# Turning q and k by transposing transfers instead of matmuls, in an attention kernel with an ELU block

## The chip, the cores and the metric

The kernel runs on one core of a Trainium2 chip. The metric is the device time of one execution in microseconds (us), as the median of several runs; lower is better.

A core has engines that each run their own instructions in order and wait for each other by semaphores. The profile calls them PE (TensorE, matmuls; its loads of stationary operands are the row PEld), DVE (VectorE), ACT (ScalarE), POOL (GpSimd) and SP (SyncE, which here only issues transfers). Transfers (DMAs) run beside them on 16 DMA engines, through one queue for SP and one for POOL. PE writes its results to PSUM, 8 banks of 2 KB in each of 128 partitions; all other on-chip data lies in SBUF.

## The reference, cut to what matters

Two attentions are computed on the same q, k and v and added: one on tokens averaged in groups of 4, whose output rows are repeated 4 times, and one local, in which a token sees only tokens at a distance under 4. The sum goes through two dense layers with an ELU between them.

```python
B, H, S, D = 8, 8, 576, 64            # batch, heads, tokens, head size
q_d = q.reshape(B, H, S // 4, 4, D).mean(axis=3)       # k_d, v_d likewise
out_up = np.repeat(sm_attn(q_d, k_d, v_d), 4, axis=2)
mask = np.abs(pos[:, None] - pos[None, :]) < 4
out_local = softmax(where(mask, q @ k.T / 8, -1e9)) @ v
x = (out_up + out_local).transpose(0, 2, 1, 3).reshape(4608, 512)
h = x @ w_in                           # 512 -> 2048
g = np.where(h > 0, h, np.exp(np.minimum(h, 0)) - 1)
return g @ w_out                       # 2048 -> 512
```

## The kernel before, in words

**Attention.** The work is cut by batch b (8) and by pair of heads j (4 in a batch). For each pair, q and k come from HBM by one transfer each into a tile `ld` (float32: 96 partitions, 2 heads, 6 blocks of 96 tokens, 64 wide). POOL casts each into a tile `c16` of 16-bit floats, in the order block, head, width (line 516). A score needs q and k with the head's width on the partitions, so each block of 96 x 128 has to be turned. Before, PE does that: a matmul with the block as the stationary operand and a constant as the moving one. The constant `ONE` has 120 columns, an identity of 96 and 24 columns that average 4 tokens each, so the same matmul also gives the averaged tokens (line 548, batches 2 to 7). ACT then copies the result from PSUM into the tiles `qt` (128 x 720), `kt` and `kd` (lines 563, 575 and 577). Batches 0 and 1 (`SIX`) load their tokens in another order, 6 neighbouring tokens on one partition, with longer pieces in HBM, and are turned with other constants (lines 536 and 540; evictions 571 and 572).

From `qt`, `kt` and `kd`, PE computes the scores: 12 matmuls for the local windows (line 620) and 4 for the averaged tokens (line 628). ACT takes the exponential of both heads (line 637), DVE multiplies with a band mask (line 644). Once a batch, PE sums the denominators with constant matrices (line 665), DVE takes the reciprocal (line 692), and from batch 2 on POOL spreads it over the partitions through a DRAM tile `rd` into `rcb` (lines 719 and 724). PE multiplies the weights with v (lines 748 and 756), DVE normalizes into `xn` (line 771), and POOL adds local and averaged outputs into `xt`, the operand of the dense layers (line 787). v is loaded into one tile of float32 and cast by POOL (lines 470 and 473).

**Dense layers.** The 4608 tokens are cut into 9 tiles of 512. A tile has 16 groups `mm1` of 4 matmuls (line 804), each followed by an exponential on ACT (line 810) and two passes on DVE (812, and 815 which writes `gt`), and 16 groups `mm2` of 4 matmuls (line 827), whose results ACT copies to `os` (842) and SP stores (845). Tile t needs the attention output of the batches whose tokens it holds: the last two tiles need batch 7.

**What sets the order.** Every operation is recorded with its engine, an assumed duration, its buffers and a rank, a due time in the units of the assumed durations. A planner (`Plan.run`) then plays the engines forward: each engine takes, among the operations that are ready and whose buffers are free, the one of lowest rank. The order that comes out is written into the program, engine by engine; on the chip each engine runs it in that order, whatever the real durations are. Ranks come from the numbers in `PARAM`: dense tile t is due from `M0 + P * t` on, the pair j of batch b from `late(b, j) = M0 + P * b - LEAD + GAP * j` on. A pair's casts have the rank `late` - 8, its transposes `late`, its scores `late` + `SC` (3.9 before), its loads `late` - `LOAD` (23.14); a batch's outputs are due `OUT` (1.4 before) ahead of the tile.

The planner also deals out the buffers (`SLOTS`): 8 of `ld`, 4 of `c16`, 3 each of `qt` and `kt` (with a `kd` each), and the PSUM banks. A pair of banks ("two") is taken by a transposed operand, by the scores of one head and by the outputs of one pair; in steady state only banks 0 to 3 serve these, and 4 to 7 the dense layers, at most 3 for `mm1` and 2 for `mm2`. SP may have 8 transfers open at a time: each waits for the one eight places earlier.

Of the kernel before, what the change touches and what calls it, by code (L numbers as in the profile page):

```python
# [11 lines left out]
FP32 = mybir.dt.float32  # L12
AB = mybir.AluOpType
AF = mybir.ActivationFunctionType

B, H, S, D = 8, 8, 576, 64
SD = S // 4
SCALE = 0.125
NB, QB = 6, 96
KW = QB + 6  # L20
VB = 112
HB = 3 * QB
# [47 lines left out]
class Plan:  # L70
# [183 lines left out]
    def emit(self):  # L254
        for o in self.order:
# [5 lines left out]
    "rcb": 2, "rc": 2, "rd": 2, "xn": 3, "xt": 3, "gt": 2, "e": 4, "os": 3,  # L261
}
MOE_BANKS = {"hp": 3, "op": 2}
PARAM = dict(M0=30, P=36.77, LAG=1.06, LEAD=53.49, GAP=7.69, SC=3.9, DEN=33.04, OUT=1.4, OUTG=1.98,
             LOAD=23.14, VLOAD=27.91, VCAST=36.99, warm=3.4, FILL=27.63, WI=-27.58, WO=38.12, WOG=2.24,
             OVER=1.0, LEAD1=57.82, GAP1=5.57, OUT1=32, VLOAD1=41.43, LOAD1=28.31, CC=-45.43, tv0=-26.96,
             C0=-7.99, SC0=2.71, OUTA=-25.9, OUTB=-21.42, DEN0=3.42, DENB=-28.86, SPA=-26.1, SPB=-20.87,
             V0=-46.5, G0=1, G1=2, G2=3, G3=3, G4=3, G5=8, G6=3, G7=13, G8=13, L0=2, L1=6, L2=0, L3=8,
             L4=0, LAG0=1.07, QG=2.08)


@with_exitstack
def kernel(
# [15 lines left out]
    def many(kind, shape, dt=FP16):  # L289
# [25 lines left out]
    def at(b):  # L315
        return T[b.kind][b.slot[0]]
# [36 lines left out]
    def fills():  # L353
        for t, x in (("ONE", 0.0), ("BY6", 0.25), ("VR", 0.25), ("MASK", 1.0), ("IND", 0.0), ("FIRST", 1.0), ("GAP", 0.0)):
            nc.vector.memset(C[t][:], x)  # L355
        nc.vector.memset(C["ONE"][:, QB:], 0.25)
        nc.vector.memset(C["VR"][:, 24:], 0.0)
        nc.vector.memset(C["IND"][:, 9:10], 1.0)
        nc.vector.memset(C["FIRST"][:, 1:10], 0.0)
        for i in range(3):  # L360
            nc.vector.memset(C["GAP"][32 * i : 32 * i + 24, 9:10], 1.0)
        for t in T["kt"]:
            nc.vector.memset(t[:, 0:3], 0.0)
            nc.vector.memset(t[:, S + 3 : S + 6], 0.0)
        for t in KD:
            nc.vector.memset(t[:], 0.0)

# [139 lines left out]
    def cast(b, j):  # L507
        s, r = st[b, j], late(b, j)
        s["c"], s["op"] = [], []
        for i, x in enumerate(s["ld"]):  # L510
# [9 lines left out]
            )  # L520
            s["c"].append(y)

    def transposes(b, j):
        s, r = st[b, j], late(b, j)
        yq, yk = s["c"]
        m = b in SIX
        con = c_a
        for which, y in (("q", yq), ("k", yk)):
            z = Buf("two", b < EARLY)

            def go(y=y, z=z):
                t = at(y)

                def natural(c):
                    o = PS[:, z.slot[0] + c // 3, 96 * (c % 3) : 96 * (c % 3) + 96]
                    nc.tensor.matmul(o, t[:, c, :, :], C["ONE"][:, 0:QB], start=True, stop=True)

                for c in range(NB):
                    if m:
                        nc.tensor.matmul(  # L540
                            PS[:, z.slot[0] + 1, HB : HB + SD], t[:, c, :, :], C["BY6"][:, c],
                            start=(c == 0), stop=(c == NB - 1),
                        )
                        if c < 3:
                            natural(c)
                    else:
                        o = PS[:, z.slot[0] + c // 3, 120 * (c % 3) : 120 * (c % 3) + 120]
                        nc.tensor.matmul(o, t[:, c, :, :], C["ONE"][:], start=True, stop=True)  # L548
                for c in range(3, NB) if m else ():
                    natural(c)  # L550

            op("PE", 0.63 if m else 0.315, r + (0 if which == "q" else 0.2), go, reads=[y], writes=[z],
               after=[con], name=f"t{which}{b}{j}")
            w = Buf("qt" if which == "q" else "kt")

            eng = "DVE" if b == 0 and which == "k" else "ACT"

            def ev(z=z, w=w, which=which, copy=nc.vector.tensor_copy if eng == "DVE" else nc.scalar.copy):
                zz = PS[:, z.slot[0], 0:1]
                if which == "q":  # L560
                    t = at(w)
                    if not m:
                        copy(  # L563
                            out=t[:].rearrange("p (g u) -> p g u", g=2), in_=_free(zz, [[512, 2], [1, 360]])
                        )
                        return
                    o, od = t[:, 0:1], t[:, S : S + 1]
                else:
                    o, od = at(w)[:, 3:4], KD[w.slot[0]][:, 0:1]
                if m:  # L570
                    copy(out=_free(o, [[1, 2 * 3 * QB]]), in_=_free(zz, [[1, QB], [512, 2], [QB, 3]]))
                    copy(out=_free(od, [[1, SD]] if which == "q" else [[32, NB], [1, 24]]),
                         in_=PS[:, z.slot[0] + 1, HB : HB + SD])
                    return
                copy(out=_free(o, [[HB, 2], [96, 3], [1, 96]]), in_=_free(zz, [[512, 2], [120, 3], [1, 96]]))  # L575
                zp = PS[:, z.slot[0], 96:97]
                copy(out=_free(od, [[QB, 2], [32, 3], [1, 24]]), in_=_free(zp, [[512, 2], [120, 3], [1, 24]]))

            op(eng, (0.72 if which == "q" else 0.9) if not m else 0.97 if eng == "DVE" else 0.86, r + 0.3, ev, reads=[z], writes=[w],
               after=[o_fill], name=f"ev{which}{b}{j}")  # L580
            s[which] = w

# [24 lines left out]

    def scores(b, j):
        s, r = st[b, j], late(b, j) + (PARAM["SC"] if b else PARAM["SC0"])
        m = b in SIX  # L610
        qb, kb = s["q"], s["k"]
        sc = [Buf("two", b < EARLY), Buf("two", b < EARLY)]

        def go():
            qt, kt, kd = at(qb), at(kb), KD[kb.slot[0]]
            for c in range(NB):
                for e in range(2):
                    p = slice(64 * e, 64 * e + 64)
                    qa = QB * c if m else 120 * c
# [309 lines left out]
```

## Time and profile before

| what | value |
|---|---|
| runs, median (lowest to highest) | 363.8 us (362.5 to 365.24, 3 runs) |
| the profiled execution, span from first to last instruction | 362.9 us; the page gives no other time of it |
| mean granted TensorE clock | 0.984 of full |
| packets on SP's queue | 108,038, 39.49 MB, 52.3% of 16 engines' span |
| packets on POOL's queue | 6,288, 8.84 MB, 13.3% |
| loads of q and k (64 in all) | 288 KB each, 5.2 and 5.4 us from issue to landing (median) |
| stores of the output (36) | 256 KB each, 2.0 us to landing |
| DVE waiting for the exponential (line 644 for 637) | 41.4 us in 28 waits |
| DVE waiting for the outputs' matmuls (line 771 for 756) | 23.8 us in 8 waits |
| SP waiting for ACT's copy to `os` before a store | 169.0 us in 30 waits |

A row of a group in the profile names line, engine, operation, output and inputs, shape and count; then the busy time of the group in us, the mean time of one in ns, and the idle time of the engine just before, with what ended it. The busy time counts overlapping instructions once, so for pipelined matmuls it is less than count times mean. "DMA" in the rows by slice is the mean busy share of the 16 DMA engines in tenths, one digit for each fortieth of the span (9.07 us); in the windows the share can exceed 1, since packets on one engine overlap. The chain of waits follows back from the last instruction to what released it, step by step.

### The profile page before, as it was taken

The numbers are of one execution on the slowest core, as the hardware profiler recorded it, in microseconds if no ns is written. First come the engines' busy times: TensorE is split into PE (matmuls) and PEld (weight loads), VectorE is DVE, ScalarE is ACT, GpSimd is POOL, SyncE is SP. The second block draws the span as 40 slices with busy tenths as digits, with TensorE's granted clock in tenths as the row PEclk, the third lists the DMA queues.
The fourth block names the chain that finished last, engine by engine and source line by source line (L and its number), as shares of the span: only waits on it lengthen the run. The fifth ranks groups of instructions, "written<-read, shape, count | busy, mean of one in ns | idle before, by whom it ended". The sixth has DMA issues, their size and how long they took to land.

```text
span 362.9 us, 8968 instructions
## 1 busy us (share of the span) xinstructions
PE 347.5 (96%) x3677; PEld 189.3 (52%) x3677; DVE 224.4 (62%) x410; ACT 211.5 (58%) x364; POOL 144.0 (40%) x226
## 2 busy tenths in 40 slices
PE   8995999999998998999999999999999999999995
PEld 7984554455454554554555455555554444444442
DVE  3658598336885597557755865398547667765510
ACT  2643696469865677557855785488557415544411
POOL 7645554277274544570557055634330160000000
PEclk9998799899999999999999999999999999999999
DMA  8999999999979799479746975103001311010021
GB/s 218 216 157 225 258 199 191 202 201 235 234 168 222 193 181 220 93 157 214 155 94 153 218 149 99 61 35 83 31 30 60 87 48 40 0 58 33 29 77 68
DMA packets 114366, 48.89 MB, mean 135 GB/s; under 512 B 100662, under 2 KB 108662, under 8 KB 114326
## 3 DMA queue, kind: packets, MB, share of 16 engines
q1 hardware_dynamic: 108038, 39.49, 52.3%
q0 software_dynamic: 6288, 8.84, 13.3%
q8 instruction: 28, 0.46, 0.6%
q14 instruction: 12, 0.10, 0.1%
HBM read 42.86 MB, written 9.66 MB: 145 GB/s over the span
## 4 chain that ended last, share of the span: by engine, by line
PE 78%; DVE 9%; ACT 6%; issue 2%; DMA 2%; POOL 2%; ACTq 0%; DVEq 0%; POOLq 0%
PE bank L827 32%; PE bank L804 27%; PE bank L548 4%; PE bank L620 3%; PE bank L748 3%; DVE e L812 3%; PE bank L329 3%; ACT e L810 2%; DVE gt L815 2%; PE bank L665 2%; ACT ex L637 2%; DVE ex L644 2%; DMA rcb<-rd 1%; PE bank L540 1%; PE bank L756 1%
## 5 line engine op out<-in xcount | busy, mean ns | idle before, releaser
L804 PE MATMUL bank<-xt,WI 128*128 128x512 f16 x576 | 141.2, 382 | 1.6 <-DVE gt L815 1.4
L827 PE MATMUL bank<-WO,gt 128*128 128x512 f16 x576 | 140.3, 381 | 1.9 <-DVE gt L815 1.9
L810 ACT ACTIVATE e<-bank 128x512 f16<-128x512 f32 x144 | 85.1, 603 | 49.1 <-PE bank L804 27.2
L815 DVE SCALAR_TENSOR_TENSOR gt<-bank,e 128x512 f16<-128x512 f32 x144 | 97.8, 688 | 4.9
L827 PEld LDWEIGHTS <-gt 128*128 128x128 f16 x576 | 54.0, 98 | 64.4 <-DVE gt L815 2.6
L804 PEld LDWEIGHTS <-WI 128*128 128x128 f16 x576 | 53.1, 98 | 64.0 <-issue 6.3
L812 DVE TENSOR_SCALAR e<-e 128x512 f16<-128x512 f16 x144 | 55.4, 386 | 39.6 <-ACT e L810 38.8
L516 POOL CAST c<-ld 96x768 f16<-96x768 f32 x60 | 50.6, 861 | 50.5 <-issue 25.7
L637 ACT ACTIVATE ex<-bank 102x864 f16<-102x864 f32 x64 | 53.4, 887 | 23.7 <-PE bank L628 23.5
L787 POOL TENSOR_TENSOR xt<-xn 128x288 f16<-128x288 f16 (+8 forms) x92 | 44.4, 514 | 54.1 <-DVE xn L771 54.0
L644 DVE TENSOR_TENSOR ex<-ex,MASK 102x1152 f16<-102x1152 f16 x32 | 28.6, 895 | 41.5 <-ACT ex L637 41.4
L842 ACT COPY os<-bank 128x512 f32<-128x512 f32 x36 | 21.3, 590 | 46.4 <-PE bank L827 43.4
L771 DVE TENSOR_TENSOR xn<-bank,rcb 128x720 f16<-128x720 f32 x32 | 27.8, 901 | 25.6 <-PE bank L756 23.8
L473 POOL CAST v<-v 102x768 f16<-102x768 f32 x32 | 27.5, 887 | 0.3 <-DMA v<-in_v_dram 0.3
L548 PEld LDWEIGHTS <-c 96*128 96x128 f16 x288 | 18.1, 97 | 8.0 <-issue 0.4
L563 ACT CAST qt<-bank 128x720 f16<-128x720 f32 x24 | 18.3, 761 | 4.2 <-PE bank L548 3.7
L548 PE MATMUL bank<-ONE,c 96*128 96x120 f16 x288 | 20.6, 216 | 0.0
L719 POOL DMA_DIRECT2D rd<-rc x6 | 3.5, 578 | 41.3 <-DVE rc L692 19.7
L329 PE MATMUL bank<-zero 128*128 128x128 f16 x221 | 17.3, 240 | 1.8 <-DVE ONE L355 1.1
L620 PEld LDWEIGHTS <-kt 64*102 64x102 f16 x384 | 11.7, 125 | 12.6 <-ACT e L810 4.7
L575 ACT CAST kt<-bank 128x576 f16<-128x576 f32 x24 | 15.6, 651 | 1.2 <-ACT qt L563 1.2
L329 PEld LDWEIGHTS <-zero 128*128 128x128 f16 x221 | 15.1, 109 | 2.4 <-DVE zero L332 1.1
(67 smaller groups left out, 228.6 us busy)
## 6 DMA issues: line engine op xcount, KB each, us to landing
ld<-in_q_dram SPq DMA_DIRECT2D x32, 288.0 KB, 5.2
ld<-in_k_dram SPq DMA_DIRECT2D x32, 288.0 KB, 5.4
out_dram<-os SPq DMA_DIRECT2D x36, 256.0 KB, 2.0
v<-in_v_dram SPq DMA_DIRECT2D x13, 672.0 KB, 8.8
rcb<-rd POOLq DMA_DIRECT2D x12, 360.0 KB, 5.6
WO<-in_moe_w_out_dram POOLq DMA_DIRECT2D x4, 512.0 KB, 9.1
WI<-in_moe_w_in_dram POOLq DMA_DIRECT2D x3, 512.0 KB, 11.3
v<-in_v_dram SPq DMA_DIRECT2D x3, 336.0 KB, 8.6
```

The costliest lines, as they stand in the source:

```text
L329: nc.tensor.matmul(PS[:, 7, 384:512], zero[:, 0:128], zero[:, 128:256], start=True, stop=True)
L516: f(out=at(y)[:], in_=at(x)[:].rearrange("p e c d -> p c e d"))
L548: nc.tensor.matmul(o, t[:, c, :, :], C["ONE"][:], start=True, stop=True)
L637: lambda e=e: nc.scalar.activation(out=at(x)[:, e], in_=two(sc[e], 0, KW, 0, HB + SD), func=AF.Exp, scale=SCALE),
L644: nc.vector.tensor_tensor(out=a, in0=a, in1=mk, op=AB.mult)
L771: lambda: nc.vector.tensor_tensor(out=at(w)[:], in0=two(z, 0, 128, 0, GW), in1=at(y)[:, j], op=AB.mult),
L787: (nc.vector if eng == "DVE" else nc.gpsimd).tensor_tensor(out=at(xt(t))[:, j, o : o + n - a], in0=ln, in1=gn, op=AB.add)
L804: nc.tensor.matmul(one(h, 0, 128, 0, TBLK), WI[:, dc, 128 * fc : 128 * fc + 128], at(x)[:, dc, :], start=(dc == 0), stop=(dc == DMC - 1),)
L810: op("ACT", 0.55, r, lambda: nc.scalar.activation(out=at(e)[:], in_=one(h, 0, 128, 0, TBLK), func=AF.Exp), reads=[h], writes=[e], name=f"e ...
L812: op("DVE", 0.42, r, lambda: nc.vector.tensor_scalar(out=at(e)[:], in0=at(e)[:], scalar1=1.0, scalar2=-1.0, op0=AB.min, op1=AB.add), reads ...
L815: op("DVE", 0.64, r, lambda: nc.vector.scalar_tensor_tensor(out=at(gt)[:, fc, :], in0=one(h, 0, 128, 0, TBLK), scalar=0.0, op0=AB.max, in1 ...
L827: nc.tensor.matmul(one(z, 0, 128, 0, DM), at(gt)[:, fc, 128 * tt : 128 * tt + 128], WO[:, fc, :], start=(fc == 0), stop=(fc == FCN - 1),)
```

## The change

From batch 2 on, q and k are no longer turned by PE. For each of them SP issues one transposing transfer from the cast tile `c16` (96 partitions, 768 elements) straight into `qt` or `kt` (128 partitions, 6 blocks of 96), both in SBUF. The averaged tokens no longer come out of the same step: DVE sums 4 neighbouring tokens, for q into the last 144 columns of `qt`, for k into `kd`, and scales all of `kd` by 1/16, which stands for both averages. The matmuls of line 548 and the copies of lines 563, 575 and 577 are gone, and with them the PSUM banks that they took. Batches 0 and 1 are turned as before.

`kt` gets a margin of `KO` = 16 columns instead of 3 on each side, zeroed at the start, so that the transfer's target is aligned; the scores read from it accordingly, and `qt` now has its 576 tokens in one piece. The transfers have the rank `late` + `TU` (-5), the sums 1.0 more. The score rank `SC` goes from 3.9 to 8.25 (batch 1 too), the outputs' lead `OUT` from 1.4 to 5.0, that of batch 1 (`OUT1`) from 32 to 26.86; the last part of `w_out` waits for an earlier cast (`G8` from 13 to 4); `VCAST` and `WO` move by under 0.3.

```diff
+KO = 16
-PARAM = dict(M0=30, ..., SC=3.9, DEN=33.04, OUT=1.4, ..., VCAST=36.99, ..., WO=38.12, ..., OUT1=32, ..., G8=13, ...)
+PARAM = dict(M0=30, ..., SC=8.25, DEN=33.04, OUT=5.0, ..., VCAST=36.92, ..., WO=38.35, ..., OUT1=26.86, ..., G8=4, ..., TU=-5.0)
...
-        "kt": many("kt", [128, S + 6]),
+        "kt": many("kt", [128, S + 2 * KO]),
...
+    def turned(b, j):
+        s, r = st[b, j], late(b, j) + PARAM["TU"]
+        for i, (which, y) in enumerate(zip("qk", s["c"])):
+            w = Buf("qt" if which == "q" else "kt")
+
+            def go(y=y, w=w, which=which):
+                t = at(w)
+                a = t[:, 0:S] if which == "q" else t[:, KO : KO + S]
+                nc.sync.dma_start_transpose(
+                    out=a.rearrange("p (c u) -> p c u", c=NB), in_=at(y)[:].rearrange("p c e d -> p (c e d)"))
+
+            op("SP", 1.5, r + 0.1 * i, go, reads=[y], writes=[w], nbytes=S * 256, rate=200e3, packet=75,
+               after=[o_fill], name=f"tu{which}{b}{j}")
+
+            def pool(w=w, which=which):
+                t = at(w)
+                if which == "q":
+                    nc.vector.tensor_reduce(out=t[:, S : S + SD], in_=t[:, 0:S].rearrange("p (u f) -> p u f", f=4),
+                                            axis=AX.X, op=AB.add)
+                    return
+                d = _free(KD[w.slot[0]][:, 0:1], [[32, NB], [1, 24]])
+                nc.vector.tensor_reduce(
+                    out=d, in_=_free(t[:, KO : KO + 1], [[QB, NB], [4, 24], [1, 4]]), axis=AX.X, op=AB.add)
+                nc.vector.tensor_scalar_mul(out=KD[w.slot[0]][:], in0=KD[w.slot[0]][:], scalar1=1.0 / 16.0)
+
+            op("DVE", 0.68 if which == "q" else 0.85, r + 1.0 + 0.1 * i, pool, reads=[w], writes=[w], name=f"po{which}{b}{j}")
+            s[which] = w
+
     def transposes(b, j):
+        if b not in SIX:
+            return turned(b, j)
...
-                        kt[p, QB * c : QB * c + KW], qt[p, qa : qa + QB], start=True, stop=True,
+                        kt[p, QB * c + KO - 3 : QB * c + KO - 3 + KW], qt[p, QB * c : QB * c + QB], start=True, stop=True,
...
-                    qd = qt[p, S : S + SD] if m else _free(qt[p, QB : QB + 1], [[120, NB], [1, 24]])
+                    qd = qt[p, S : S + SD]
```

In the order that the planner writes from these numbers, a batch's eight transposing transfers stand on SP's queue between loads of the next batch and stores of finished output rows.

More of the change, by code (lines that the diff above doesn't have):

```diff
@@ L14 @@
 AF = mybir.ActivationFunctionType
+AX = mybir.AxisListType
 B, H, S, D = 8, 8, 576, 64
@@ L362, in fills @@
         for t in T["kt"]:
-            nc.vector.memset(t[:, 0:3], 0.0)
-            nc.vector.memset(t[:, S + 3 : S + 6], 0.0)
+            nc.vector.memset(t[:, 0:KO], 0.0)
+            nc.vector.memset(t[:, S + KO : S + 2 * KO], 0.0)
         for t in KD:
@@ L538, in go @@
                 for c in range(NB):
[L539 to L549, printed above, removed]
+                    nc.tensor.matmul(
+                        PS[:, z.slot[0] + 1, HB : HB + SD], t[:, c, :, :], C["BY6"][:, c],
+                        start=(c == 0), stop=(c == NB - 1),
+                    )
+                    if c < 3:
+                        natural(c)
+                for c in range(3, NB):
                     natural(c)
-            op("PE", 0.63 if m else 0.315, r + (0 if which == "q" else 0.2), go, reads=[y], writes=[z],
+            op("PE", 0.63, r + (0 if which == "q" else 0.2), go, reads=[y], writes=[z],
                after=[con], name=f"t{which}{b}{j}")
@@ L609, in scores @@
         s, r = st[b, j], late(b, j) + (PARAM["SC"] if b else PARAM["SC0"])
-        m = b in SIX
         qb, kb = s["q"], s["k"]
```

32 lines of the change are left out of this document (10 added, 22 removed).

## The prediction

> **What bounds the kernel now.** I read the busy shares first, then the groups that the change touches, the windows by stage, the chain of waits, and the landings of the transfers.
>
> ```profile
> PE 347.5 (96%) x3677; PEld 189.3 (52%) x3677; DVE 224.4 (62%) x410; ACT 211.5 (58%) x364; POOL 144.0 (40%) x226
> ...
> DMA  8999999999979799479746975103001311010021
> ...
> PE 78%; DVE 9%; ACT 6%; issue 2%; DMA 2%; POOL 2%; ACTq 0%; DVEq 0%; POOLq 0%
> ...
> L548 PE MATMUL bank<-ONE,c 96*128 96x120 f16 x288 | 20.6, 216 | 0.0
> ```
>
> TensorE is busy 96% of the span, and the transposes of batches 2 to 7 (L548) are 20.6 us of that. The DMA row says the other thing to keep in mind: nearly full until about slice 12 (110 us), uneven until slice 24 (220 us), almost empty after.
>
> ```profile
> 98.00:134.00 36.00, 34.37 (x389) 17.87 (x388) 25.66 (x37) 22.84 (x41) 20.30 (x31) 1.00 0.94 192
> 134.00:171.00 37.00, 35.88 (x398) 18.62 (x397) 24.12 (x42) 23.89 (x42) 17.29 (x27) 1.00 0.92 172
> 171.00:207.00 36.00, 36.00 (x398) 18.83 (x398) 23.17 (x42) 24.16 (x42) 17.40 (x27) 1.00 0.73 152
> 207.00:244.00 37.00, 37.00 (x410) 19.20 (x405) 22.97 (x39) 25.16 (x44) 17.82 (x28) 1.00 0.40 94
> 244.00:281.00 37.00, 37.00 (x401) 19.05 (x399) 24.30 (x44) 24.69 (x43) 10.61 (x19) 1.00 0.17 51
> ```
>
> Each window holds about one batch; the columns are the window's length, busy time of PE, PEld, DVE, ACT and POOL, the granted clock, the DMA share and GB/s. PE has no gap from 171 to 281 us and loses about 1.6 and 1.1 us in the two windows before. So what is taken from PE there is time, as long as nothing else comes late. In the four windows from 134 us (147 us) DVE is busy 94.6 us, 23.6 per batch of 36.75.
>
> **PE: what goes.** 6 batches x 4 pairs x 2 operands x 6 matmuls = 288, which cover 20.6 us (71.5 ns each, 3.43 per batch). The new transfers do all of their work. In the chain of waits L548 holds 3.6% of the span, 13.1 us; the other 7.5 us lay where the chain ran through another engine. So the gain on PE lies between 13.1 and 20.6, before new waits. The score matmuls keep their count and sizes; their operands only lie elsewhere: nothing.
>
> **ACT: what goes.** The evictions of these transposes, the first two rows as the page has them and the third as the groups by shape have it:
>
> ```profile
> L563 ACT CAST qt<-bank 128x720 f16<-128x720 f32 x24 | 18.3, 761 | 4.2 <-PE bank L548 3.7
> ...
> L575 ACT CAST kt<-bank 128x576 f16<-128x576 f32 x24 | 15.6, 651 | 1.2 <-ACT qt L563 1.2
> ```
> ```profile
> L577 ACT CAST kd<-bank 128x144 f16<-128x144 f32 x24 | 7.2, 302 | 0.0
> ```
>
> 41.1 us leave ACT, 6.9 per batch of some 24.5. ACT has 6% of the chain, and it idles a third of each window, so I count nothing for it directly; it makes the exponentials of both halves come sooner. PE also waited 3.0 us in all for the last of these evictions (L620 for kd). That wait turns into one for VectorE's sums, so I don't count it either.
>
> **DVE: what comes.** Per pair one sum of 576 elements to 144 for q, the same for k, and a scaling of 198 elements. No such sum is in the trace. From below: the fp16 pass over 512 elements (L812) has a median of 293 ns; from above, a 576-element cast out of PSUM on this engine takes 755 ns (L571). I take 700 ns, near the upper row, as the sum also reads 576 elements. The scaling lies between nothing and 296 ns (L572, 144 elements from PSUM); I take 200. That is 1.6 us a pair (0.6 to 1.8), 6.4 a batch, 38 in all. DVE goes from 23.6 to 30.0 us a batch, while PE's own work falls from 36.75 to 33.3: DVE is then 90% busy, and is the engine that is late next.
>
> **SP and the DMA queue: what comes.** 48 transfers of 144 KB. Issue on SP: a q load's issue (L444) takes 0.31 to 5.7 us, 0.4 to 1.0 in the median; I take 1.0, so 8 us a batch. SP issued for about 17 us of the 37 from 134 on, so there is room. On the queue: a source of 96 rows in 6 blocks of 256 bytes is 576 packets. The page's 52.3% for 108,038 packets is 362.9 x 0.523 x 16 / 108,038 = 28.1 ns a packet, so 576 x 28.1 / 16 = 1.0 us per transfer. From below, 144 KB at the best slice's 258 GB/s is 0.57 us; from above, the whole landing time of a k load, 5.4 us. I take 1.0, as the packets have the size of the loads' packets: 8 us a batch, 48 in all. What the shares leave free from 98 to 281 us is 2.2 + 3.0 + 9.7 + 22.2 + 30.7 = 68 us, 1.4 us for each of 48 transfers; in the two tight windows (134 to 207) it is 12.7 us for 16, 0.8 each. At 1.0 the queue just holds them, with some loads later than now.
>
> The Trainium skill speaks on both sides. VectorE: DVE Perf Modes, "The three transpose paths", gives 390 ns for a 128x128 transpose on TensorE and 1309 ns on the DMA crossbar; by it, 4.5 such blocks would hold the queue an estimated 5.9 us. Advanced Engine Details and Errata, "X-Bar Transpose (TRN2)", says that transposing DMAs are as fast as regular ones, 350 to 400 GB/s, an estimated 0.4 us here. No row of before has such a transfer; by the second the queue has room, by the first it is far too full, which is the third rival below.
>
> **The new waits.** A sum on DVE waits for its transfer to land, and behind it in DVE's order stand the ELU passes that feed PE. On SP a transpose waits for POOL's cast and for a free kt buffer; behind it stand the next loads and stores, and the store before it waits for ACT (30 such waits, 169 us in all). On POOL a cast now waits until the transfer two pairs back has landed, ahead of the adds that fill xt. Loads had 23 units of lead in the written order; between transfer and scores there are 13. The landings show how uneven transfers are:
>
> ```profile
> DMA to landing us min/median/max: 3.0/5.2/11.5
> ```
>
> That is L444's answer. Below, these waits cost nothing: the order leaves room for them. Above, each pair is late by what a median load is later than the fastest, 2.2 us, 53 us for 24 pairs. Between them I take what PE lost when the transfers were crowded: from 60 to 171 us it idled 1.5 + 1.6 + 1.1 = 4.2 us in three windows, 1.4 each; for six batches 8.5 us.
>
> **Sum.** 362.9 - 20.6 + 8.5 = 350.8 us of span. A second way agrees: DVE's 30.0 us plus its wait for the exponentials (41.4 us over 8 batches, 5.2 each) is 35.2 a batch, 1.55 under 36.75, so 9.3 us of gain and 353.6. The middle is 352. The page gives no time but the span; the median of the runs is 0.9 above it: **352 to 353, and I say 352**. The order of batch 1 and one weight load (WO's last part, issued earlier) move too; they add no work and lie before 100 us, where PE is covered by fills and weights: between -1.5 and +1.5 us (the idle time of the window from 60), counted zero.
>
> What is late next at the end: the last two tiles need batch 7. In the chain and the timeline the reciprocal of its denominators starts at 280.06 us, the DMA that spreads it lands at 289.3, the last normalization ends at 296.6, and the first matmul of those tiles starts at 298.14; 64 groups of four matmuls at 0.865 us, 55.4 us, can only come after that. PE fills these 18 us with 18 groups of older tiles and the outputs. In the changed order only 16 groups stand there, 1.7 us less, so PE may wait that long once; the 8.5 us cover it. Otherwise batch 7 comes sooner by what the batches before it save, as its place in the order is set against the same tiles.
>
> **Rivals.**
>
> 1. DVE becomes the bound and the gain is lost. For: 90% busy. If its wait for the exponentials stays (5.2) and half of that for the outputs (23.8 / 8 / 2 = 1.5), a batch takes 36.7, as now: 363. Against: with 6.9 us a batch gone from ACT, the first wait must shrink. Chance 0.13, 359 to 367.
>
> 2. Slower: DVE, in order, stands before a sum whose transfer hasn't landed, and the ELU passes behind it hold PE. The point from which it decides is 20.6 / 24 = 0.86 us a pair, beyond what the buffers take up. At 1.5 us a pair it is 362.9 - 20.6 + 36 = 378; at 2.2, 395. For: landings vary by more than that, and SP's single order ties a transfer to a store and so to PE's own progress. Against: once everything has shifted, the transfers run ahead again, and the three banks for h let PE go on for three groups of 0.865 us, 2.6 us. Chance 0.21, 367 to 395.
>
> 3. The crossbar is slow, or the transfer falls apart into small pieces, so that the change doesn't do what it says cheaply: above 1.4 us per transfer the queue has no room (the 68 us). At 2.2 us: 48 x 0.8 = 38 us more than the gaps hold, 380 and above; at the load's 5.4 us, 48 x 4.0 = 192 us more, some 535. Against: the bytes are half a load's. Chance 0.11, above 388.
>
> **How the numbers follow.** Forecast 0.55 (341 to 359, from 20.6 with no new wait, 343.2, to hardly any gain). A measurement tells about 1% from no change here (the runs span 362.5 to 365.2). Faster 0.55, same 0.13, slower 0.32. The range must reach into rival 2; 341 to 388 leaves out rival 3, a little of rival 2's upper end and a few hundredths below.
>
> **What would show it.** Right: L548's matmuls of 96x120 gone and PE's busy time near 327; ACT near 170, DVE near 260; PE's idle time between 98 and 281 us near 8 us, with DVE's gt as its releaser; DVE's sums at 0.7 us. Wrong: sums on DVE that wait for transfers in long pieces, clock drops after 100 us, transfers with landings beyond 6 us, a DMA row that stays at 9 until 280 us.

## The result and the profile after

The changed kernel is slower by 1%: a median of 368.8 us (364.8 to 373.8, 18 runs) beside 363.6 us (362.4 to 367.7, 18 runs) of the kernel before on the same chips, a ratio of 1.0101 with the 95% interval 1.0069 to 1.0134. Ratios, here and below, leave out disturbed runs, so they are not the quotient of the medians. The profiled execution has a span of 367.1 us, 4.2 more than the one of before. The forecast was 352 us.

The page of the kernel after, first the lines that answer to those shown of before, and three groups (line, engine, operation, count; busy us, mean ns of one; idle time before and what ended it):

```profile
PE 336.1 (92%) x3389; PEld 175.6 (48%) x3389; DVE 262.6 (72%) x482; ACT 181.4 (49%) x292; POOL 148.4 (40%) x226
...
DMA  8999999999999999999999999969010401011011
...
q1 hardware_dynamic: 137222, 46.57, 69.0%
...
PE 55%; DVE 17%; DMA 12%; issue 6%; POOL 3%; SPq 3%; ACT 3%; POOLq 0%; DVEq 0%; ACTq 0%
...
L819 PE MATMUL bank<-xt,WI 128*128 128x512 f16 x576 | 141.9, 383 | 11.0 <-DVE gt L830 10.2
...
L542 DVE TENSOR_REDUCE qt<-qt 128x144 f16<-128x576 f16 x24 | 17.8, 740 | 0.0
L546 DVE TENSOR_REDUCE kd<-kt 128x144 f16<-128x576 f16 x24 | 17.7, 740 | 0.0
```

The change did to the engines much of what it says: ACT went from 211.5 to 181.4 us, DVE from 224.4 to 262.6. But PE's busy time fell by 11.4 us only, not by the 20.6 of the removed group, and PE's time without work (span minus busy) went from 15.4 to 31.0 us: 15.6 more, so that the span grew by 4.2. PE is no longer almost the whole chain (78%, now 55%); DVE and the transfers have taken its place in it, DMA from 2% to 12%. The DMA row, uneven before from slice 12 on, is now full until slice 26 (239 us).

The same stages as in the windows of before (length; busy time of PE, PEld, DVE, ACT, POOL with counts; granted clock; DMA share; GB/s):

```profile
98.00:134.00 36.00, 31.67 (x350) 15.46 (x350) 29.48 (x50) 18.96 (x30) 18.49 (x28) 1.00 1.19 207
134.00:171.00 37.00, 34.82 (x348) 16.44 (x347) 31.79 (x57) 19.73 (x31) 20.22 (x30) 0.95 1.12 204
171.00:207.00 36.00, 32.30 (x342) 15.65 (x340) 32.19 (x54) 18.46 (x29) 19.51 (x29) 1.00 1.24 202
207.00:244.00 37.00, 34.82 (x353) 16.73 (x352) 33.57 (x58) 20.25 (x33) 18.69 (x27) 1.00 1.15 194
244.00:281.00 37.00, 35.38 (x430) 17.31 (x429) 30.09 (x55) 19.67 (x32) 10.78 (x19) 1.00 0.33 67
```

PE idles 4.3 + 2.2 + 3.7 + 2.2 + 1.6 = 14.0 us from 98 to 281 us, where it idled 2.8 before. DVE is busy 29 to 34 us in a window, up from 23 to 26. The DMA share of the second to the fourth window was 0.92, 0.73 and 0.40; now it is 1.12 to 1.24.

The waits of the kernel after (who waits for whom: us in total, times, longest) show what comes late:

```profile
POOL v L475 <- DMA v<-in_v_dram: 22.6, 11, 6.2
...
PE bank L819 <- DVE gt L830: 10.2, 13, 1.9
...
DVE xn L786 <- DMA rcb<-rd: 8.6, 4, 2.7
```

Before, PE's `mm1` waited 1.4 us for `gt`, POOL's cast of v 0.3 us for its load, and DVE's normalization 1.2 us for `rcb`. One piece of the chain, in order of time (start, length, what), shows how these hang together between 159 and 224 us:

```profile
159.03 0.95 SPq L472
160.03 10.33 DMA v<-in_v_dram
...
175.55 3.24 DMA rd<-rc
180.56 1.61 POOL c L518 x2
182.38 1.20 SPq L533
184.30 1.24 SPq L533
185.63 2.25 SPq L533
187.94 1.57 SPq L446
189.56 1.35 SPq L446
190.95 0.98 SPq L472
191.98 9.42 DMA v<-in_v_dram
...
210.94 5.53 DMA rd<-rc
217.37 6.80 DMA rcb<-rd
```

L533 is the new transfer's issue. SP issues three transposes, two loads and then the load of v, one after the other; the load of v takes 9.4 us to land, and the denominators' way through DRAM (`rd`, `rcb`) 5.5 and 6.8 us more. In the whole chain of before, transfers had 2%, some 7 us. The issues themselves, in the answer for the transfer's line (duration in ns min/median/max, first and last start, and the landings):

```profile
L533 SPq DMA_TRANSPOSE qt<-c x24: 1197/1397/6484, 68.5 to 252.3; - x24
L533 SPq DMA_TRANSPOSE kt<-c x24: 1195/1212/2771, 72.7 to 253.6; - x24
...
DMA to landing us min/median/max: 2.5/4.5/10.0
```

### The profile page after: what moved, and what is told of

It is laid out like the page before. It is cut to its first block, busy times and chain, and to the rows that moved or that the text cites. A ratio compares the mean times of both kernels' runs of the same rounds, so it can differ in the third digit from the quotient of the medians.

```text
span 367.1 us, 8470 instructions
## 1 busy us (share of the span) xinstructions
PE 336.1 (92%) x3389; PEld 175.6 (48%) x3389; DVE 262.6 (72%) x482; ACT 181.4 (49%) x292; POOL 148.4 (40%) x226
## 3 DMA queue, kind: packets, MB, share of 16 engines
q1 hardware_dynamic: 137222, 46.57, 69.0%
## 4 chain that ended last, share of the span: by engine, by line
PE 55%; DVE 17%; DMA 12%; issue 6%; POOL 3%; SPq 3%; ACT 3%; POOLq 0%; DVEq 0%; ACTq 0%
PE bank L842 24%; PE bank L819 21%; DMA v<-in_v_dram 5%; DVE e L827 4%; DVE gt L830 3%; DMA rd<-rc 2%; DMA ld<-in_q_dram 2%; DVE kd L546 2%; PE bank L763 2%; DMA rcb<-rd 2%; DVE qt L542 2%; DVE kd L548 2%; DVE ex L659 2%; PE bank L680 1%; PE bank L570 1%
## 5 line engine op out<-in xcount | busy, mean ns | idle before, releaser
L830 DVE SCALAR_TENSOR_TENSOR gt<-bank,e 128x512 f16<-128x512 f32 x144 | 96.8, 685 | 4.0
L819 PEld LDWEIGHTS <-WI 128*128 128x128 f16 x576 | 54.9, 98 | 78.4 <-issue 17.9
L518 POOL CAST c<-ld 96x768 f16<-96x768 f32 x60 | 52.7, 907 | 22.4 <-DMA ld<-in_q_dram 8.5
L475 POOL CAST v<-v 102x768 f16<-102x768 f32 x32 | 29.2, 935 | 22.6 <-DMA v<-in_v_dram 22.6
L659 DVE TENSOR_TENSOR ex<-ex,MASK 102x1152 f16<-102x1152 f16 x32 | 26.9, 841 | 14.7 <-ACT ex L652 14.3
L635 PEld LDWEIGHTS <-kt 64*102 64x102 f16 x384 | 11.8, 124 | 12.9 <-issue 12.6
L542 DVE TENSOR_REDUCE qt<-qt 128x144 f16<-128x576 f16 x24 | 17.8, 740 | 0.0
L546 DVE TENSOR_REDUCE kd<-kt 128x144 f16<-128x576 f16 x24 | 17.7, 740 | 0.0
L635 PE MATMUL bank<-qt,kt 64*102 64x96 f16 x384 | 16.0, 214 | 0.5 <-DVE xn L786 0.5
L570 PE MATMUL bank<-BY,c 96*128 96x144 f16 x96 | 11.1, 233 | 5.6 <-DVE xn L786 4.4
## 6 DMA issues: line engine op xcount, KB each, us to landing
v<-in_v_dram SPq DMA_DIRECT2D x3, 336.0 KB, 8.0
```

Of the source, the lines that this page charges most:

```text
L475: nc.gpsimd.tensor_copy(out=at(x)[:, j].rearrange("p e c d -> p (e c) d"), in_=at(x32)[0:KW, 12 * j : 12 * j + 12, :])
L518: f(out=at(y)[:], in_=at(x)[:].rearrange("p e c d -> p c e d"))
L659: nc.vector.tensor_tensor(out=a, in0=a, in1=mk, op=AB.mult)
L819: nc.tensor.matmul(one(h, 0, 128, 0, TBLK), WI[:, dc, 128 * fc : 128 * fc + 128], at(x)[:, dc, :], start=(dc == 0), stop=(dc == DMC - 1),)
L830: op("DVE", 0.64, r, lambda: nc.vector.scalar_tensor_tensor(out=at(gt)[:, fc, :], in0=one(h, 0, 128, 0, TBLK), scalar=0.0, op0=AB.max, in1 ...
```

## The experiments

All medians and ratios first. "Idle" is span minus PE's busy time in the profiled execution.

| kernel | median us | ratio to before, 95% | span | PE busy | idle |
|---|---|---|---|---|---|
| before | 363.6 | | 362.9 | 347.5 | 15.4 |
| after | 368.8 | 1.0101 (1.0069 to 1.0134) | 367.1 | 336.1 | 31.0 |
| e1_no_sums | 367.5 | 1.0091 (1.0049 to 1.0134) | 364.3 | 334.5 | 29.8 |
| e2_sixth | 374.0 (367.1 to 378.0) | none | 373.1 | 339.0 | 34.1 |
| e3_both | 364.2 | 1.0015 (0.9983 to 1.0047) | 359.0 | 334.9 | 24.1 |
| e4_from5 | 368.6 | 1.0108 (1.0029 to 1.0186) | 363.3 | 341.8 | 21.5 |
| e5_none | 360.3 | 0.9900 (0.9872 to 0.9929) | 358.0 | 334.5 | 23.5 |
| d_sums | 372.7 | 1.0266 (1.0216 to 1.0316) | 372.9 | 349.3 | 23.6 |
| d_transfers | 372.2 | 1.0243 (1.0189 to 1.0297) | 369.5 | 347.2 | 22.3 |
| n_before_newnum | 376.9 | 1.0387 (1.0340 to 1.0435) | 373.6 | 350.4 | 23.2 |
| i_alone | 385.2 | one run | 383.5 | | |
| f_one_mm | 360.2 | 0.9904 (0.9876 to 0.9933) | 358.2 | 335.7 | 22.5 |
| f_light_dve | 361.4 | 0.9941 (0.9911 to 0.9972) | 357.8 | 336.0 | 21.8 |
| g_light_dve | 364.1 | 0.9993 (0.9955 to 1.0030) | 362.3 | 346.3 | 16.0 |
| f_replan | 356.0 | 0.9789 (0.9714 to 0.9864) | 356.9 | 334.4 | 22.5 |
| h_567 | 370.5 | 1.0153 (1.0098 to 1.0209) | 368.5 | 344.6 | 23.9 |

### The parts of the change, taken out of the changed kernel

The first theories put the loss on the queue (A), on DVE's sums (B), or on neither, but on the waits in order on SP and DVE for the landing (C). Three kernels in the order of the changed one are to tell them apart: without the sums, with a sixth of each transfer, and with both cuts.

**Without the sums.** One column is copied in place of each sum, and nothing is scaled; the averaged tokens of batches 2 to 7 are left out.

```diff
-                    nc.vector.tensor_reduce(out=t[:, S : S + SD], in_=t[:, 0:S].rearrange("p (u f) -> p u f", f=4), ...)
+                    nc.vector.tensor_copy(out=t[:, S : S + 1], in_=t[:, 0:1])
...
-                nc.vector.tensor_reduce(out=d, in_=_free(t[:, KO : KO + 1], ...), axis=AX.X, op=AB.add)
-                nc.vector.tensor_scalar_mul(out=KD[w.slot[0]][:], in0=KD[w.slot[0]][:], scalar1=1.0 / 16.0)
+                nc.vector.tensor_copy(out=KD[w.slot[0]][:, 0:1], in_=t[:, KO : KO + 1])
```

> The changed kernel in its own order, but each of VectorE's 48 sums copies one column instead (and the scaling is gone): the averaged tokens of batches 2 to 7 are left out; each copy still waits for its transfer to land. It takes some 43 us from VectorE. Theory A (the DMA queue is full because of the transposing transfers, and loads, v and the spread of the reciprocals come late): little changes, 364 to 369. Theory B (VectorE, 90% busy with the sums, holds PE): 350 to 357. Theory C (neither, but waits in order on SP and VectorE for the landing): 363 to 369.

DVE lost 33.0 us of work (262.6 to 229.6), and the ratio stayed: 1.0091 beside 1.0101, with intervals that overlap almost wholly. So B alone falls: while the transfers stand, DVE's load is not what costs the time. The waits of this kernel name the transfers instead:

```profile
POOL v L477 <- DMA v<-in_v_dram: 22.9, 10, 7.1
...
DVE xn L784 <- DMA rcb<-rd: 15.5, 4, 5.9
...
ACT os L855 <- DMA out_dram<-os: 9.0, 3, 4.0
```

**A sixth of each transfer.** Each turns one block of six into its place; the other five blocks of a batch's q and k are left unturned (the buffers are zeroed once at the start).

```diff
-                    out=a.rearrange("p (c u) -> p c u", c=NB), in_=at(y)[:].rearrange("p c e d -> p (c e d)"))
+                    out=a[:, 0:QB], in_=at(y)[:, 0].rearrange("p e d -> p (e d)"))
```

> The changed kernel in its own order, but each transposing transfer turns one block of 96 tokens instead of six: a sixth of the bytes on the queue, as many issues on SP, the same waits; the scores of the other blocks use stale data. The sums stay. Theory A: the DMA shares after 98 us fall back to about those of the kernel before (0.9 to 0.2), PE idles under 8 us between 98 and 281 us, 350 to 358. Theory B: no change, 364 to 369. Theory C: a little from the shorter landing, 360 to 366.

Its queue fell back to 53.2% of 16 engines' time, where before has 52.3%. Of its four runs only the fastest, 367.1 us, can be set beside the others, so no ratio is given. It lies above before's median (363.6) and among the runs of the changed kernel (364.8 to 373.8): no gain is seen from the bytes alone while the sums are there, which speaks against A alone, on one run.

**Both cuts.** What is left of the change are the 48 issues, small transfers, the wait for their landing, and two small copies a pair.

> Both cuts at once: a sixth of the bytes, and one column instead of the sums. What is left is the changed order, the issues on SP and the waits for landing. Theories A and B both: 345 to 352, near the full gain of PE (20.6 us of matmuls in the profile, or 11 if the fall of PE's busy time in the changed kernel is the right size, then 350 to 353). Theory C: 358 or more.

1.0015: as fast as before, and faster than without the sums alone (1.0091) and, as far as its one run tells, than with a sixth alone. So the two loads together cost something. But 364 us is C's range, far from the 345 to 353 of A and B: with transfers and sums cut to almost nothing, PE's removed work still brought nothing. In this kernel DVE shows the wait that was feared, as it has little else to do there:

```profile
DVE qt L544 <- DMA qt<-c: 9.9, 7, 2.2
...
DVE kd L546 <- DMA kt<-c: 5.5, 6, 3.1
```

15.4 us of DVE's time went into waiting for transfers to land. So the remaining question was what PE's matmuls had been worth.

**No transfers at all.** As the last one, without the issues; the small copies read from the cast tile, so only the cast is waited for. q and k of batches 2 to 7 are left unturned.

```diff
-                t = at(w)
-                a = t[:, 0:S] if which == "q" else t[:, KO : KO + S]
-                nc.sync.dma_start_transpose(...)
+                pass
...
-                    nc.vector.tensor_copy(out=t[:, S : S + 1], in_=t[:, 0:1])
+                    nc.vector.tensor_copy(out=t[0:QB, S : S + 1], in_=at(y)[:, 0, 0, 0:1])
```

> The changed kernel in its own order with no transfers at all and one column instead of the sums, which waits for the cast alone: nothing is turned, the scores of batches 2 to 7 use stale data. Beside the run with a sixth of the bytes and no sums (364) it shows what the issues on SP and the waits for landing cost by themselves. Theory C (they hold that version): 350 to 356. If instead the order that was planned around the transfers and the sums, with its places for them, is what holds it: 360 to 365.

0.9900; 360.3 us is the range of the second case, in which the order holds the time, and not of theory C. This is the most that the change could bring in its own order: 1.0%, 3.6 us, if turning and averaging cost nothing at all. From there the parts add up in steps: small transfers with their issues and waits cost 1.15% (4.2 us), the other five sixths of the bytes 0.8% (2.8 us), the sums 0.1% (0.4 us, within the intervals). The steps hold in this succession only: with the sums in place, the cut of the bytes brought nothing in its one run.

### What PE's matmuls were worth

**One of six.** The kernel before in its own order, with one transposing matmul for each operand in place of six; the copies keep their sizes and copy the first block six times, so five of six blocks are left out. 240 of 288 matmuls are gone; nothing is added and nothing moved.

```diff
-                    else:
+                    elif c == 0:
                         o = PS[:, z.slot[0] + c // 3, 120 * (c % 3) : 120 * (c % 3) + 120]
                         nc.tensor.matmul(o, t[:, c, :, :], C["ONE"][:], start=True, stop=True)
...
-                            out=t[:].rearrange("p (g u) -> p g u", g=2), in_=_free(zz, [[512, 2], [1, 360]])
+                            out=t[:].rearrange("p (c u) -> p c u", c=NB), in_=_free(zz, [[0, NB], [1, 120]])
```

> The kernel before in its own order with one of the six matmuls per operand (240 of 288 gone): five blocks of q and k are left out, and the evictions, as many and as long as before, copy the first block six times. It asks what the transposes are worth on PE with nothing put in their place. By the group's busy time (71.5 ns each) 17.2 us: 346. By the interval from one to the next in the timeline (0.31 us for six, 52 ns each) 12.5 us: 351. If other engines take the place at once, as in the changed kernel: 355 or more.

0.9904, 3.5 us. The page of this kernel:

```profile
PE 335.7 (94%) x3437; PEld 176.0 (49%) x3437; DVE 224.2 (63%) x410; ACT 209.7 (59%) x364; POOL 147.1 (41%) x226
```

PE's busy time fell by 11.8 us, and its idle time grew by 7.1. The new idle time stands at one wait, as the waits show, first of the kernel before, then of this one:

```profile
PE bank L804 <- DVE gt L815: 1.4, 2, 1.1
```
```profile
PE bank L804 <- DVE gt L815: 7.0, 8, 1.6
```

So 5.6 us of wait, beside 7.1 us more idle time, went to `mm1` waiting for DVE's `gt`: with the transposes gone, PE comes sooner to the next group and stands before a result that is no earlier than before. The matmuls had filled time in which PE would have waited.

**Is it DVE's load that holds `gt`?** The multiplication with the band mask, 0.9 us a pair on DVE, is cut to 8 of 288 columns for batches 2 to 7 (the local band is left out), once with one of six matmuls and once in the kernel before.

```diff
-            a = at(x)[:, :, :, 0:HB]
-            mk = _free(C["MASK"][:], [[0, 2], [HB, 2], [1, HB]])
+            w = HB if b in SIX else 8
+            a = at(x)[:, :, :, 0:w]
+            mk = _free(C["MASK"][:], [[0, 2], [HB, 2], [1, w]])
```

> As the kernel before with one of six matmuls per operand (360), in its order, and VectorE's mask pass of batches 2 to 7 cut to 8 of 288 columns (the local band is left out): some 15 us less on VectorE. If PE, with its transposes gone, waits for VectorE: 350 to 356. If not for VectorE: 358 to 361.

> The kernel before with all its transposes and only the mask pass cut to 8 columns. If PE's work bounds the kernel before, lighter work on VectorE is worth at most PE's 4 us of gaps: 360 to 364. If VectorE's passes bound it: 350 to 358.

0.9941 and 0.9993: no gain over 0.9904 and over 1. The test is weaker than meant: a pass went from 0.90 to 0.29 us, 14.6 us for 24 of them, but DVE's sum fell by 7.1 only (224.2 to 217.1), as the first pass of the ELU grew from 55.1 to 60.3 us. With the 33 us of the run without sums beside it, the sum of DVE's load is still hardly the cause. As little points at ACT's: without transfers (e5_none) ACT has 181 us of work where the kernel with one of six has 210, and both come out at 0.990, though in different orders.

**What holds `gt`, by the trace.** DVE's first ELU pass (L812) has a median of 0.293 us. In the kernel with one of six it takes 2.04, 1.67 and 1.67 us ahead of the three longest waits of `mm1` (1.65, 1.28 and 1.28 us, at 135.5, 172.0 and 208.6 us; together 4.2 of the 7.0 us). In each of the three places POOL runs two casts of q and k, one behind the other, and the pass ends 0.15 us after the second. The first of them, from the timelines of DVE, POOL and PE:

```profile
132.70 2.04 DVE L812 TENSOR_SCALAR e<-e 128x512 f16<-128x512 f16 x1 [0.59 <-ACT e L810]
132.99 1.60 POOL L516 CAST c<-ld 96x768 f16<-96x768 f32 x2
134.78 0.69 DVE L815 SCALAR_TENSOR_TENSOR gt<-bank,e 128x512 f16<-128x512 f32 x1
135.52 1.02 PE L804 MATMUL bank<-xt,WI 128*128 128x512 f16 x4 [1.65 <-DVE gt L815]
```

All 20 of the 144 passes that take over 0.4 us lie beside an instruction of POOL for at least 69% of their time and end 0.15 to 0.21 us after one; of the other 124, 33 touch one at all. In the kernel before, the pass in the first place is as long (2.04 us), and PE waits 1.1 us there. In the other two places it takes 0.91 us, as there POOL leaves 0.20 us between the two casts, and PE does not wait. So the longest waits come from passes that stretch while POOL works, and a lighter mask pass does not shorten those. No run moves the casts, so what their places cost in time is not measured.

**Is it the order?** One of six again, but the planner is told that these matmuls take a sixth of their time, and writes the order anew.

```diff
-            op("PE", 0.63 if m else 0.315, r + (0 if which == "q" else 0.2), go, reads=[y], writes=[z],
+            op("PE", 0.63 if m else 0.0525, r + (0 if which == "q" else 0.2), go, reads=[y], writes=[z],
```

> As the kernel before with one of six matmuls per operand (360), but the planner is told that they take a sixth of the time, so the order is written for it. If the freed time is lost because the order still keeps places for the transposes: 348 to 355. If it is lost to the engines that PE then waits for (VectorE's ELU passes, which free the banks): 357 to 363.

0.9789 (0.9714 to 0.9864), twice the gain; 356.0 us lies between the two ranges. Part of the freed time is lost because the instructions keep their places, and part comes back when they are placed anew; even so the gain, 7.7 us, is a good third of the 20.6 us. How much of the doubling is the right order and how much luck of one order is not settled, as the next run shows that orders differ by more than that.

### The parts, added to the kernel before

**Only the ordering numbers.** The kernel before with the new `PARAM`, and nothing else.

> The kernel before with the changed kernel's ordering numbers (SC 8.25, OUT 5.0, OUT1 26.86, G8 4 and the small ones) and nothing else. If the numbers by themselves cost the time that is missing: 367 to 372. If they are harmless: 361 to 366.

1.0387, beyond both ranges. The numbers are made for the changed work and harm the old one; they do not help by themselves. No work was added, and 14 us were lost: the order of the instructions alone can cost more than the whole change did.

**Only the sums.** The kernel before, with the same sums and scaling into a tile that nobody reads.

```diff
+            def extra(w=w, which=which, j=j):
+                t, x = at(w), SX[(2 * j + (which == "k")) % 4]
...
+                nc.vector.tensor_reduce(out=x[:, 0:SD].rearrange("p (c u) -> p c u", c=NB), in_=src, axis=AX.X, op=AB.add)
+                if which == "k":
+                    nc.vector.tensor_scalar_mul(out=x[:], in0=x[:], scalar1=1.0 / 16.0)
```

> The kernel before, turned by matmuls as it was, with the sums alone added: after each eviction of batches 2 to 7 VectorE also sums 4 neighbours into a spare tile (and scales it for k), which nothing reads; the order is planned anew with them. Theory D (in the changed kernel VectorE's load and the transfers' load are each enough to hold PE, so that taking away one gains nothing): VectorE rises from 224 to some 267 us, PE gets gaps, 367 to 374. If VectorE's load does no harm by itself: 362 to 366.

**Only the transfers.** The kernel before, with the 48 transfers into a tile that nobody reads.

```diff
+                def extra(y=y, x=x):
+                    nc.sync.dma_start_transpose(
+                        out=at(x)[:].rearrange("p (c u) -> p c u", c=NB), in_=at(y)[:].rearrange("p c e d -> p (c e d)"))
```

> The kernel before with the transfers alone added: for batches 2 to 7 SP also turns each cast tile into a spare tile that nothing reads; PE still turns them too; the order is planned anew. Theory D: loads and v come late, 367 to 375, DMA shares over 1 from 98 to 244 us. If the queue's load does no harm by itself, and only the waits for the landing do: 362 to 366.

1.0266 and 1.0243, in the ranges of theory D. Either burden, with its new order, costs some 2.5% where PE is full, but both were planned anew with the old numbers, and the run with the new numbers says how much a mere new order can cost. So they price neither burden, and tell the two apart as little as the cuts do.

**The transfer alone.** 16 of them behind the last store, with nothing else on the queue.

> The kernel before, and after its last store 16 transposing transfers of a cast tile into 4 spare tiles, one behind the other with nothing else on the queue; nothing reads them. Their time per transfer is what one holds the queue without other traffic: 1.0 us by the packets' mean in the profile before, 0.57 us by bytes at the best slice's rate, 1.2 us if SP's issue (1.2 us in the changed kernel) is what limits; then the whole is some 17 to 25 us longer than the kernel before.

The timeline of SP at the end of this kernel, and the answer for the line:

```profile
358.40 1.20 SPq L846 DMA_DIRECT2D out_dram<-os  x2
359.69 21.08 SPq L901 DMA_TRANSPOSE sx<-c  x16
```
```profile
L901 SPq DMA_TRANSPOSE sx<-c x16: 1203/1265/1330, 359.7 to 379.5; - x16
...
DMA to landing us min/median/max: 2.5/2.6/2.7
```

21.08 / 16 = 1.32 us each, from issue to issue, and SP is held for 1.27 of them. The queue isn't what limits them, as the DMA view of the last 24.5 us shows (packets, MB, share of 16 engines):

```profile
q1 hardware_dynamic: 10016, 2.89, 53.7%
```

53.7% of 24.5 us is 13.2 us for 16 transfers and the rest of a store: at most 0.8 us of the queue each. In the changed kernel the queue's packets took 0.690 x 367.1 = 253.3 us, before 0.523 x 362.9 = 189.8: 63.5 us for 48 transfers, 1.3 us each in company.

### Fewer transfers

**From batch 5 on**, where the queue had room; batches 2 to 4 are turned by PE with the old numbers.

```diff
+BY_DMA = (5, 6, 7)
...
-        if b not in SIX:
+        if b in BY_DMA:
             return turned(b, j)
```

> The change for batches 5, 6 and 7 alone; batches 2 to 4 are turned by matmuls as before, with the old score and output ranks; the order is planned anew. The transfers of these batches fall after some 170 us, where the kernel before had DMA shares of 0.73, 0.40 and 0.17. Theory A: the queue has room, half of PE's gain stays, 355 to 360. Theory B: VectorE is as full in these batches as in the changed kernel, no gain, 361 to 366. Theory C: 361 to 367.

1.0108 (368.6 us, above all three ranges) for half of the transfers, as much as for all. The same with the measured durations given to the planner (issue 1.25, sums 0.74 and 1.05) and the ranks searched anew:

> Batches 5 to 7 alone by transfers, as in the earlier mixed kernel, but planned with what was measured for the new operations (1.25 us of SP, 1.29 us of the queue, 0.74 and 1.05 us of VectorE) and with ranks searched anew for that. If the order, written for costs that the chip doesn't have, is what takes the gain: 353 to 360. If the queue and VectorE themselves take it in these batches too: 362 to 368.

1.0153, above both ranges. No version with transfers beat the kernel before.

## Why the prediction was wrong

**PE: what goes (20.6 us, at least 13.1). This step failed.** Three errors lie in it. First, the busy time of a group of small matmuls is not the time that PE needs for it: a matmul's row reaches into the next one's. In the timeline of before one set of six has a row of 0.48 us, but the next group starts 0.31 us after it:

```profile
134.39 0.48 PE L548 MATMUL bank<-ONE,c 96*128 96x120 f16 x6
134.70 1.03 PE L804 MATMUL bank<-xt,WI 128*128 128x512 f16 x4
135.57 0.48 PE L548 MATMUL bank<-ONE,c 96*128 96x120 f16 x6
```

So 48 sets take some 15 us. Busy time fell by 11.4. An estimate from the same rows covers most of the other 3.7: the group of 1.03 us is followed by the next after 0.87 us, so where PE waits behind such a group instead, 0.16 us more count as busy. The trace after has 36 idle stretches of PE, the one before 14, and 22 x 0.16 is 3.5 us. The Trainium skill, Perfetto Trace Analysis, "Identifying the Most-Contended Engine", says that the busy share of matmuls is not a good measure of how close PE is to its limit, because pipelined instructions look smaller in the trace. The trace agrees that it is a poor measure; here a group looked larger than its worth, 20.6 us beside 11.4 of the sum. Second, the share in the chain of waits is no lower bound of a gain. It says what ended last, not how close behind the next thing was; here `gt` was close behind. Third, "PE has no gap, so what is taken from it is time" is true only if what it waits for comes sooner as well, and `gt` did not: ahead of the longest waits it stood behind DVE passes that stretch beside POOL's casts. With the matmuls removed and nothing added, 3.5 us came out in the old order (f_one_mm) and 3.6 in the new one (e5_none).

**The sum with this term alone replaced** is 362.9 - 3.6 + 8.5 = 367.8 us of span; measured were 367.1. The rest of the sum was near in size, though not in its reasons.

**The new waits (8.5 us).** From e5_none to the changed kernel the ratio goes from 0.9900 to 1.0101, 7.3 us. The size was near, in part by luck: 8.5 was taken from PE's idle time between 60 and 171 us before, within bounds of 0 and 53. The place was right in part: 4.2 us come with the issues and the waits for landing, even where the transfers are small, 2.8 us with the bytes and 0.4 with the sums.

**SP and the queue (1.0 us each on both).** SP is held 1.2 to 1.4 us in the median and 6.5 at worst, and a transfer takes 1.3 us of the queue in company, at most 0.8 alone. The room of 1.4 us per transfer was computed rightly and was used up: the DMA row stays full until 239 us, and the loads of v, `rcb` and the stores come late, as the waits and the chain show. The price by 576 packets at the 28.1 ns of before was short: there are 608 to a transfer (1.07 us), and the mean of all the queue's packets rose to 29.5 ns (253.3 x 16 / 137,222), on the loads and stores too. This is as far as the third rival goes (it put the threshold at 1.4): the queue got full, but nothing collapsed. The figure behind it, 1309 ns for a block of 128x128 and so an estimated 5.9 us for a transfer (the Trainium skill, VectorE: DVE Perf Modes, "The three transpose paths"), does not agree: 0.8 us is measured. The other rule, that such a transfer is as fast as a regular one (the Trainium skill, Advanced Engine Details and Errata, "X-Bar Transpose (TRN2)", an estimated 0.4 us), is nearer for the queue but leaves out the 1.27 us in which SP issues it.

**DVE: what comes (38 us, 1.6 a pair).** DVE grew by 38.2 us. A sum takes 0.740 us where 0.70 was taken; the scaling has a mean of 0.484 us, not 0.20. The three groups have 17.8 + 17.7 + 11.6 = 47.1 us, so the total was met by luck, with two durations too small and a count that, as on PE, forgot that groups overlap their neighbours (the mask pass also fell by 1.7 us). That DVE would be late next was right as a place (`gt` releases PE) and not shown as a cause: 33 us less on DVE, with the transfers left in, changed the ratio by 0.1%.

**ACT (41.1 us, counted at nothing).** The runs agree with counting it at nothing, without a test of it alone: f_one_mm with these copies and e5_none without them are equally fast, but in different orders. The groups of 41.1 us were 30.1 us of ACT's busy time, the same overlap again.

**The rivals.** The first, that the gain is lost, had the releaser (`gt`) and nearly the size (359 to 367, measured 368.8), but its reason, the sum of DVE's load, is not borne out by e1_no_sums and f_light_dve. The second, slower by DVE standing before a sum whose transfer hasn't landed, had the sign, and its range (367 to 395) holds the time; its wait shows in e3_both (15.4 us on DVE), but not in the changed kernel, where the sums have no idle time before them. Its point of decision, 0.86 us a pair, was built on the 20.6 us; on 3.6 it would have been 0.15 us a pair, which nothing in the profile could have excluded. That is how one mis-sized term turned the sign: the case for slower was priced against a gain five times too big.

**What would show it.** PE's busy time near 327 (336.1) and idle time near 8 us from 98 to 281 us (14.0) were both missed; ACT near 170 (181), DVE near 260 (262.6), `gt` as the releaser and the sums at 0.7 us came out so or nearly so. Of the signs for wrong, two came: landings beyond 6 us (10.0 at most) and a DMA row that stays at 9, if to 239 us and not 280. A third came in one window: the granted clock is 0.95 from 134 to 171 us, where before has 1.00. It explains little, as the two dense groups of PE grew by 0.9 us in all (281.5 to 282.4).

What stays open: how much of the lost gain would come back if POOL's casts stood in other places. The trace shows them beside the passes that hold `gt`, less load on DVE did not help, and a new order recovered some of it; no run moves the casts alone.

## What to carry to other kernels

Work taken from an engine that is 96% busy in a written order is worth what the next-latest result allows, not its busy time: here five sixths of a group of 20.6 us were 11.8 us of busy time and 3.5 us of time. Before moving work elsewhere, take it away without replacing it, in the same order: that run gives the most that the move can bring in this order, and all its costs (issue, queue, waits) have to fit into it. And a change that is measured together with a new order must be set against how much an order alone can move, here 3.9%.

## What the runs showed of the hardware

The issue of a transposing transfer from SBUF to SBUF held SP for 1.27 us (median) with nothing else under way, and still for 1.1 to 1.2 us with a sixth of the bytes (e3_both), so its cost hardly follows the size:

```profile
L535 SPq DMA_TRANSPOSE qt<-c x24: 1097/1211/4876, 67.5 to 245.9; - x24
L535 SPq DMA_TRANSPOSE kt<-c x24: 1092/1108/2335, 72.6 to 247.1; - x24
```

The transfer comes in small packets: 137,222 - 108,038 = 29,184 more on the queue, 608 for each of 48. And DVE's scaling of 128x198 16-bit elements took between 215 and 2377 ns, with the same shape each time. The ten of 24 with no instruction of POOL beside them took 215 to 217 ns; the 14 others, all beside one, took 216 to 2377:

```profile
L548 DVE TENSOR_SCALAR kd<-kd x24: 215/307/2377, 83.6 to 263.7; 128x198 f16<-128x198 f16 x24
```
